# A decode step of grouped-query attention beside a Mish layer: where the mid-run rows of wo are put, and in how many transfers the last eight come

## The chip, the core and the metric

The kernel runs on one core of one Trainium2 chip. The metric is the device time of one execution in microseconds (us); lower is better. A core has TensorE (PE, with its weight loads as PEld), VectorE (DVE), ScalarE (ACT), GpSimd (POOL) and SyncE (SP). SP computes nothing here: it issues almost all of the kernel's DMA transfers, in program order, and waits on semaphores between them. The transfers run on 16 DMA engines that the profile sums up as one row.

## What is computed

One decode step for a batch of 8 with model width 512: layer norm, attention of 32 query heads over 8 cached key and value heads of 8192 positions each, and beside it a dense layer with Mish and a second dense layer. Everything is fp32.

```python
def reference(A_x, A_k_cache, A_v_cache, A_wq, A_wo, B_x, B_w1, B_b1, B_w2):
    xn = _layernorm(A_x, axis=-1)
    # _A_ref: q = xn @ wq, 32 heads of 128; k, v repeated 4 times over the 8 cached heads
    scores = jnp.einsum("bhqd,bhkd->bhqk", q, k) * (Dh ** -0.5)
    o = jnp.einsum("bhqk,bhkd->bhqd", _softmax(scores, axis=-1), v)
    a = o.transpose(0, 2, 1, 3).reshape(B, Sq, Hq * Dh) @ wo
    # _B_ref
    h = jnp.einsum("bsd,df->bsf", xn, w1) + b1
    m = jnp.einsum("bsf,fd->bsd", h * jnp.tanh(softplus(h)), w2)
    return A_x + a + m
```

The caches are the bulk of the data: keys and values are 268 MB each, against 24 MB of weights.

## The kernel before

The work is cut into 32 units (`UNITS`), one for each of 4 pairs of key/value heads (`m`) and each of 8 batch rows (`b`). Unit j loads 8.39 MB of keys and 8.39 MB of values, each as one transfer of 128 partitions by 64 KB (`load_unit`, L136 to L144). Keys have two places in the large tile `kv`, values one (`V_AT`). In step j of the loop (L563 to L604) the PE multiplies the keys of unit j (`scores`), the softmax is made, the PE multiplies the values of unit j-1 (`values`), and then SP is told to load the values of unit j into the place just freed; the keys of unit j+1 are told off in the middle of `scores`. So two to three such transfers are always under way or queued.

The output projection wo is 8.39 MB, 2.1 MB for each pair of heads. It is loaded at the end (L607 to L612) into the place of the last values and keys, as rows of 16 KB in 128 partitions, and used by `outputs`; w2 follows in five pieces (L613 to L619). Of the first pair's wo only three quarters are loaded then (`n = 3 * BW`). The last quarter, 512 KB, comes during the run instead, as 32 rows of 16 KB, into partitions 0 to 11, 32 to 43 and again 0 to 7 of the tile `ws`, which is free once the last part of wq has been used. These rows are the subject:

- `FEW1` (L69) lists eight transfers of three rows, `(p, n, q, at)`: partition, rows, number of the first row, step. With h = 0 or 1 and t = 0 to 3 they are told off two to a step in steps 22 to 25.
- `FEW2` (L70) lists four transfers of two rows, two in step 28 and two in step 29.
- The loop tells them off right behind the step's value load (L591 to L593) by `load_few` (L482 to L488). Row q + 4i goes to partition p + 4i: both sides are walked with a stride of four. A row is four pieces of 4 KB in HBM and one run of 16 KB in its partition.
- `turn_few` (L490) lays the first pair's attention output out in the same order of rows, in unit 9's step. `few(0)` (L508) multiplies the first 44 partitions at the end of step 27 (`EARLY`), before the last eight rows overwrite partitions 0 to 7; `few(1)` multiplies those eight after the loop.

SP's queue is one, so a small transfer stands behind the value load issued just before it and ahead of the next key load.

Of the kernel before, what the change touches and what calls it, by code (L numbers as in the profile page):

```python
# [65 lines left out]

FEW1 = [(32 * h + t, 3, 12 * h + t, 22 + (4 * h + t) // 2) for h in range(2) for t in range(4)]  # L69
FEW2 = [(t, 2, 24 + t, 28 + t // 2) for t in range(4)]  # L70
EARLY = 27


# [4 lines left out]
def kernel(  # L78
# [21 lines left out]
    ws = const.tile([P, CC * BW], F32, name="ws")  # L100
# [381 lines left out]
    def load_few(p, n, q):  # L482

        rows = wo[:4].rearrange("u p f -> (u p f)").rearrange("(u q i f) -> q u i f", u=4, i=4, f=BW)
        nc.sync.dma_start(
            ws[p : p + 4 * n - 3 : 4].rearrange("p (u f) -> p u f", u=4),
            rows[q : q + 4 * n - 3 : 4, :, 3],
        )  # L488

    def turn_few():  # L490
# [72 lines left out]
    for j in range(UNITS):  # L563
# [25 lines left out]
        if j == 0:  # L589
            mish(w1_t, b1_sb, kv[:, W1_AT : W1_AT + 6 * FG])  # L590
        for p, n, q, at in FEW1 + FEW2:  # L591
            if j == at:
                load_few(p, n, q)  # L593
# [14 lines left out]
    for m in range(NP):  # L608
        rows = wo[4 * m : 4 * (m + 1)].rearrange("u p f -> (u p f)")
        rows = rows.rearrange("(p f) -> p f", p=P)  # L610
        n = 3 * BW if m == 0 else 4 * BW
# [4 lines left out]
    for lo, hi in parts:  # L616
        t = kv[:, W2_AT + lo * D : W2_AT + hi * D]
# [64 lines left out]
```

## Time and profile before

| | us |
|---|---|
| median of 3 runs | 1310.62 (1310.28 to 1311.18) |
| profiled execution, its own time | 1310.38 |
| its span, first to last instruction | 1308.6 |
| PE busy | 987.5 |
| DVE busy | 362.0 |
| ACT busy | 39.3 |
| mean rate of the DMA engines | 429 GB/s |

The page gives each engine's busy time, the span in 40 slices, the DMA queues, the chain of work that ended last, and groups of instructions by line. The DMA view of a window counts the packets that start in it: a packet is one contiguous piece on one DMA engine (64 KB for keys and values, 4 KB for the small rows), and the 4-byte packets are the completions that an engine posts when its part of a transfer is done. "Under 512 B" is therefore a count of completions, and "under 8 KB" less "under 2 KB" counts, in the middle of the run, the pieces of the small rows. The share can pass 100% in a short window, since a packet that starts in it is counted whole.

### The profile page before, as it was taken

The numbers are of one execution on the slowest core, as the hardware profiler recorded it, in microseconds if no ns is written. First come the engines' busy times: TensorE is split into PE (matmuls) and PEld (weight loads), VectorE is DVE, ScalarE is ACT, GpSimd is POOL, SyncE is SP. The second block draws the span as 40 slices with busy tenths as digits, with TensorE's granted clock in tenths as the row PEclk, the third lists the DMA queues.
The fourth block names the chain that finished last, engine by engine and source line by source line (L and its number), as shares of the span: only waits on it lengthen the run. The fifth ranks groups of instructions, "written<-read, shape, count | busy, mean of one in ns | idle before, by whom it ended". The sixth has DMA issues, their size and how long they took to land.

```text
span 1308.6 us, 11317 instructions
## 1 busy us (share of the span) xinstructions
PE 987.5 (75%) x5086; PEld 349.0 (27%) x5086; DVE 362.0 (28%) x771; ACT 39.3 (3%) x89; POOL 2.3 (0%) x10
## 2 busy tenths in 40 slices
PE   6967777768878668786878677688796777777677
PEld 4322222223322222232323222232232222222222
DVE  3443022230233332123331232312322330322321
ACT  1000000000000000000000000000000000000000
POOL 0000000000000000000000000000000000000000
PEclk9989888798889899878999888888897898887898
DMA  9999999999999999999999999999999999999997
GB/s 404 441 429 433 433 433 430 431 441 428 435 431 434 433 431 433 431 431 437 425 443 422 443 419 443 429 433 433 426 437 430 438 434 425 441 419 443 423 429 334
DMA packets 11608, 561.80 MB, mean 429 GB/s; under 512 B 1308, under 2 KB 1440, under 8 KB 1960
## 3 DMA queue, kind: packets, MB, share of 16 engines
q1 hardware_dynamic: 11536, 561.06, 99.3%
q8 instruction: 40, 0.66, 0.2%
q14 instruction: 8, 0.07, 0.0%
q10 hardware_dynamic: 24, 0.02, 0.0%
HBM read 561.01 MB, written 0.07 MB: 429 GB/s over the span
## 4 chain that ended last, share of the span: by engine, by line
DMA 79%; PE 20%; issue 0%; SPq 0%; DVE 0%
DMA kv<-in_v 74%; PE o L399 19%; DMA kv<-in_kT 2%; DMA kv<-in_w 2%; DMA kv<-in_wo 2%; PE s L329 1%; PE o L546 0%; SPq L134 0%; DVE os L642 0%
## 5 line engine op out<-in xcount | busy, mean ns | idle before, releaser
L329 PE MATMUL s<-kv,wk 128*64 128x512 f32 x2048 | 502.2, 653 | 180.8 <-DMA kv<-in_kT 180.8
L399 PE MATMUL o<-kv,pt 128*32 128x512 f32 x2048 | 264.5, 675 | 57.4 <-DMA kv<-in_v 57.4
L329 PEld LDWEIGHTS s<-kv,wk 128*64 128x64 f32 x2048 | 164.7, 151 | 495.0 <-issue 413.6
L341 DVE TENSOR_REDUCE nm<-s 128x1 f32<-128x512 f32 x32 | 22.1, 692 | 515.1 <-PE s L329 515.1
L368 PE MATMUL x<-e,perm 128*128 128x512 f32 x256 | 130.1, 655 | 2.0 <-ACT qr L299 2.0
L399 PEld LDWEIGHTS o<-kv,pt 128*32 128x32 f32 x2048 | 69.4, 122 | 226.1 <-issue 175.7
L407 DVE TENSOR_SCALAR os<-o,isel 128x128 f32<-128x128 f32 x32 | 11.2, 351 | 278.2 <-PE o L399 278.2
L379 DVE STREAM_TRANSPOSE tr<-x 128x512 f32<-128x512 f32 x128 | 79.2, 676 | 3.0 <-PE x L368 3.0
L368 PEld LDWEIGHTS x<-e,perm 128*128 128x128 f32 x256 | 50.6, 208 | 74.7 <-issue 72.0
L312 DVE TENSOR_TENSOR wk<-qr,mask 128x512 f32<-128x512 f32 (+1 forms) x66 | 63.5, 1003 | 18.7 <-ACT qr L299 18.7
L360 ACT ACTIVATE e<-s,nmx 128x512 f32<-128x512 f32 x32 | 22.0, 687 | 1119.8 <-DVE nmx L357 1119.8
L388 DVE TENSOR_TENSOR pt<-tr 64x512 f32<-64x512 f32 x64 | 43.9, 686 | 1.6
L384 DVE TENSOR_TENSOR tr<-tr 128x1024 f32<-128x1024 f32 x32 | 39.2, 1226 | 1.1
L409 DVE SCALAR_TENSOR_TENSOR os<-o,isel,os 128x128 f32<-128x128 f32 x96 | 33.7, 351 | 3.4
L342 PE MATMUL m<-ident,nm 128*1 128x128 f32 x32 | 8.6, 270 | 25.3 <-DVE nm L341 25.3
L353 PE MATMUL m<-ident,nx 1*128 1x1 f32 x32 | 7.0, 218 | 24.1 <-DVE nx L349 24.1
L292 PE MATMUL x<-qT,tr 128*128 128x64 f32 x128 | 19.3, 315 | 3.0 <-ACT qr L299 2.7
L292 PEld LDWEIGHTS x<-qT,tr 128*128 128x128 f32 x128 | 18.1, 226 | 6.2 <-ACT qr L299 3.3
L342 PEld LDWEIGHTS m<-ident,nm 128*1 128x1 f32 x32 | 2.5, 79 | 53.5 <-DVE nm L341 53.5
L363 DVE TENSOR_SCALAR lsel<-rsel,l 128x8 f32<-128x8 f32 x32 | 7.4, 231 | 28.8 <-ACT e L360 28.8
L416 PE MATMUL m<-hsel,os 128*128 128x8 f32 x64 | 10.9, 242 | 5.7 <-DVE rt L376 5.7
L416 PEld LDWEIGHTS m<-hsel,os 128*128 128x128 f32 x64 | 10.8, 189 | 15.3 <-issue 8.0
(106 smaller groups left out, 178.8 us busy)
## 6 DMA issues: line engine op xcount, KB each, us to landing
ws<-in_wq SPq DMA_DIRECT2D x4, 2048.0 KB, 22.6
kv<-in_wo SPq DMA_DIRECT2D x3, 2048.0 KB, 24.1
kv<-in_w SPq DMA_DIRECT2D x1, 3584.0 KB, 35.8
kv<-in_wo SPq DMA_DIRECT2D x1, 1536.0 KB
kv<-in_w SPq DMA_DIRECT2D x1, 1280.0 KB
kv<-in_w SPq DMA_DIRECT2D x1, 1024.0 KB
kv<-in_w SPq DMA_DIRECT2D x1, 768.0 KB, 34.9
kv<-in_kT SPq DMA_DIRECT2D x32, 29.4
```

The costliest lines, as they stand in the source:

```text
L292: nc.tensor.matmul(X[:, half, k * 64 : (k + 1) * 64], wide[:, half * 8 + k], qT, start=True, stop=True,)
L312: nc.vector.tensor_mul(w[:, i : i + n, d], q[:, i : i + n, d].to_broadcast([P, n, NH * G, REP]), mask[:, d * NH * G : (d + 1) * NH * G] .r ...
L329: nc.tensor.matmul(S[64 * c : 64 * (c + 1), :], w[:, i].rearrange("p d k h -> p (d k h)"), kk[:, i, c, :], start=(part == 0 and n == 0), s ...
L341: nc.vector.tensor_reduce(nm, S, axis=AX.X, op=ALU.max, negate=True)
L360: nc.scalar.activation(e, S, AF.Exp, bias=nmx, accum_out=l)
L368: nc.tensor.matmul(X[:, g], perm[:, g], e, start=True, stop=True)
L379: nc.vector.transpose(tr.rearrange("p (l t) c -> p t l c", t=TL)[:, tl], X.rearrange("p g (t q l) -> p t l g q", t=TL, q=PP)[:, tl],)
L384: nc.vector.tensor_add(t[:, :, 0], t[:, :, 0], t[:, :, 1])
L388: nc.vector.tensor_add(pt8[half, :, :, d * REP : (d + 1) * REP].rearrange("p c y h -> p y c h"), t[:, 0], t[:, 1],)
L399: nc.tensor.matmul(O[Q * q : Q * (q + 1), :], pt8[:, c, TL * l : TL * (l + 1), :].rearrange("p t h -> p (t h)"), vt[:, 512 * n : 512 * (n ...
L409: nc.vector.scalar_tensor_tensor(os, O[:, DH * i : DH * (i + 1)], isel[:, i : i + 1], os, op0=ALU.mult, op1=ALU.add)
L416: nc.tensor.matmul(M[:, 168 : 168 + H2], os, hsel, start=True, stop=True)
```

## The change

`load_few` walks partitions and rows without a stride: row q + i goes to partition p + i. The lists are rewritten to suit. `FEW1` still has eight transfers of three rows in the same steps, now to three neighbouring partitions. `FEW2` has two transfers of four rows, one in step 28 and one in step 29, each to four neighbouring partitions. Each of the 32 rows goes to the same partition as before, so `turn_few` and `few` stay as they are; which rows share a transfer, and how many transfers there are (ten instead of twelve), is what differs.

```diff
-FEW1 = [(32 * h + t, 3, 12 * h + t, 22 + (4 * h + t) // 2) for h in range(2) for t in range(4)]
-FEW2 = [(t, 2, 24 + t, 28 + t // 2) for t in range(4)]
+FEW1 = [(32 * h + 3 * t, 3, 12 * h + 3 * t, 22 + (4 * h + t) // 2) for h in range(2) for t in range(4)]
+FEW2 = [(4 * t, 4, 24 + 4 * t, 28 + t) for t in range(2)]
...
         rows = wo[:4].rearrange("u p f -> (u p f)").rearrange("(u q i f) -> q u i f", u=4, i=4, f=BW)
         nc.sync.dma_start(
-            ws[p : p + 4 * n - 3 : 4].rearrange("p (u f) -> p u f", u=4),
-            rows[q : q + 4 * n - 3 : 4, :, 3],
+            ws[p : p + n].rearrange("p (u f) -> p u f", u=4), rows[q : q + n, :, 3]
         )
```

## The prediction

> **What bounds the kernel now.** I read the page's DMA rows first, then the chain of waits, then one long window, then the DMA view of short windows around the transfers that change.
>
> ```profile
> span 1308.6 us, 11317 instructions
> ...
> DMA packets 11608, 561.80 MB, mean 429 GB/s; under 512 B 1308, under 2 KB 1440, under 8 KB 1960
> ...
> q1 hardware_dynamic: 11536, 561.06, 99.3%
> ...
> DMA 79%; PE 20%; issue 0%; SPq 0%; DVE 0%
> ```
>
> The chain that ended last is DMA for 79% of the span; the PE pieces in it (20%) are the waits of one value tile for its place. The SP queue's packets fill 99.3% of the time of 16 DMA engines.
>
> ```profile
> core 0: us, PE busy (x) PEld busy (x) DVE busy (x) ACT busy (x) POOL busy (x), PEclk, DMA share, GB/s
> 100.00:1200.00 1100.00, 829.89 (x4176) 289.44 (x4172) 298.55 (x623) 28.80 (x68) 0.00 (x0) 0.88 1.00 433
> ```
>
> Over 1100 us the DMA share is 1.00 at 433 GB/s: none of the 16 engines is ever without work, and one engine moves 433 / 16 = 27.1 GB/s. So the kernel ends when the DMA engine with the most work has done it, and the question is only what the change does to the time that each engine spends.
>
> ```profile
> 917.18 29.90 DMA kv<-in_v
> 947.08 0.04 issue
> 947.12 7.12 PE o L399 x64
> 954.24 0.02 issue
> 954.26 31.52 DMA kv<-in_v
> ```
>
> The chain of waits between 900 and 1000 us shows the cover. A value load of 8.39 MB (128 rows of 64 KB) needs 8.39 / 433 = 19.4 us, but it lands 29.90 us after its issue: some 10.5 us of earlier work stands ahead of it. A late engine therefore always finds its next transfer queued. What it loses is not made good later, and what a leading engine loses costs nothing until it has become the last.
>
> **The transfers that change.** A completion record is 4 bytes, and the page counts 1308 packets under 512 B.
>
> ```profile
> ws<-in_wo SPq DMA_DIRECT2D x8, 48.0 KB
> ws<-in_wo SPq DMA_DIRECT2D x4, 32.0 KB
> ...
> kv<-in_x ACTq DMA_DIRECT2D x1, 16.0 KB
> kv<-in_b ACTq DMA_DIRECT2D x1, 7.0 KB
> ```
>
> 79 transfers of full height on SP's queue (64 of keys and values, 4 of wq, 4 of wo, 1 of w1, 5 of w2, the output) at 16 completions are 1264. x has 8 rows and b1 has 4: 12 more. 1308 - 1264 - 12 = 32 = 8 x 3 + 4 x 2: a small transfer of n rows runs on n engines, one row each. Which engines these are is in no row; I take them to be the same first ones each time, since otherwise no single engine would stand out as it does below.
>
> One row is 16 KB in four pieces of 4 KB, so 16,384 B / 27.1 GB/s = 0.61 us on its engine. Before, engines 0 and 1 take 8 + 4 = 12 such rows each and engine 2 takes 8. After, by counting rows, engines 0 to 2 take 8 + 2 = 10 each, and a fourth engine takes 2.
>
> Now the end. The three lines below are the DMA view's packet counts for 1211 to 1219.7 us, 1219.08 to 1219.66 us and 1304.2 to 1304.8 us.
>
> ```profile
> DMA packets 97, 4.06 MB, mean 467 GB/s; under 512 B 20, under 2 KB 20, under 8 KB 36
> ```
>
> ```profile
> DMA packets 10, 0.41 MB, mean 699 GB/s; under 512 B 1, under 2 KB 1, under 8 KB 4
> ```
>
> ```profile
> DMA packets 7, 0.01 MB, mean 20 GB/s; under 512 B 1, under 2 KB 1, under 8 KB 7
> ```
>
> In the first, all 20 completions of the value load issued at 1189.65 us (16; its row stands below) and of the two small transfers behind it (2 x 2) fall. In the second, the last of the 20 stands alone, with three 4 KB pieces before it: the engine that carries the last small row is the last of all, by about 0.57 us. In the third, again one engine alone still has six 2 KB pieces and a completion of the last weights while the rest are done, again for about 0.57 us (its completion is at the window's end, the others' are before 1304.2). Same lead: **the engine that sets the end is one of the two that carry 12 rows.** What is added to it moves the end one for one; what is taken from it is worth at most 0.57 us.
>
> **The change, part by part.** (1) Two issues fewer on SP.
>
> ```profile
> 1149.15 0.33 SPq L140 DMA_DIRECT2D kv<-in_v  x1
> 1149.53 1.36 SPq L485 DMA_DIRECT2D ws<-in_wo  x2
> 1170.11 0.33 SPq L140 DMA_DIRECT2D kv<-in_kT  x1
> 1189.65 0.33 SPq L140 DMA_DIRECT2D kv<-in_v  x1
> 1190.03 1.33 SPq L485 DMA_DIRECT2D ws<-in_wo  x2
> ```
>
> One issue in place of two saves about 0.7 us of SP at steps 28 and 29, but SP's next instruction of weight, the key load, comes 20 us later and waits for PE: nothing. Were that cover gone, it would be worth 0.7 us each.
>
> (2) When the rows are used.
>
> ```profile
> L511 PE MATMUL h<-ws,oF x32: 587/589/593, 1116.4 to 1289.4; 44*8 44x512 f32 x16, 8*8 8x512 f32 x16
> L485 SPq DMA_DIRECT2D ws<-in_wo x12: 619/706/902, 917.6 to 1190.7; - x12
> ```
>
> ```profile
> DMA packets 64, 1.54 MB, mean 513 GB/s; under 512 B 18, under 2 KB 18, under 8 KB 42
> ```
>
> The last of the first 24 rows move between 1060 and 1063 us (the count above: 42 - 18 = 24 pieces of 4 KB) and are used from 1116.4. The last eight land by 1219.66, and their 16 matmuls of 0.59 us, the last begun at 1289.4, begin near 1280. A delay of some us is covered by 53 and 60 us: nothing. The matmuls read the same partitions as before.
>
> (3) Row counts alone: engines 0 and 1 lose two rows, -1.21 us each, of which the end can feel -0.57.
>
> (4) **Neighbouring partitions.** Before, the rows of one transfer go to partitions t, t+4, t+8; after, to three or four that lie side by side, written by different engines at once. No transfer of this kind of size is in the trace. That several engines are in them at once is seen in 939.9 to 942.4 us, where the first two are moved:
>
> ```profile
> DMA packets 53, 1.15 MB, mean 459 GB/s; under 512 B 13, under 2 KB 13, under 8 KB 37
> ```
>
> 37 - 13 = 24 pieces of 4 KB, 6 rows on three engines in about 2.1 us, where each engine needs 1.21: they overlap, but start up to 0.8 us apart. The lower bound of the price is nothing: rows side by side run as these do. The upper bound is that all rows of a transfer go one after another: 3 x 0.61 for each of FEW1's, so 4 pairs x (6 - 2) x 0.605 = +9.7, and 4 x 0.61 for each of FEW2's two, 4.84 against 2.42 before = +2.4; together +12.1.
>
> The nearest row is x's load, the one in which several engines write side by side (8 rows of 2 KB to partitions 0 to 7). The window 1.69 to 2.7 us holds all its packets:
>
> ```profile
> q1 hardware_dynamic: 14, 0.23, 109.4%
> q10 hardware_dynamic: 15, 0.02, 10.1%
> ```
>
> 10.1% of 16 x 1.01 us is 1.63 us; less 7 completions (under 0.1) that is 0.19 us a row, where 2,048 B / 27.1 is 0.076: 2.6 times. Four writers served in turn at one engine's rate give a mean of (1+2+3+4)/4 = 2.5, eight give 4.5, two 1.5. I take groups of **four partitions that share one path of one engine's rate**. Against it: in the same window the first wq packets, 14 of 16 KB, took 17.7 us, 1.26 each against 0.61, twice as long with no such neighbours, so part of the 2.6 may be the start. It is an estimate from a weak row.
>
> [...]
>
> Worked out: at each of steps 22 to 25 the six rows are partitions 0,1,2 then 3,4,5 (or 6,7,8 then 9,10,11, and the same 32 higher). One group of four gets four rows, 4 x 0.605 = 2.42 us through one path, where each engine now spends 2 x 0.605 = 1.21: +1.21 a step, 4 steps, **+4.8** (taken in full, though the 0.8 us apart may hide a part). At steps 28 and 29 four rows go into one group: 2 x 2.42 = 4.84 against the 4 x 0.605 = 2.42 that engines 0 and 1 spend now, +2.42 if all four arrive together, 2 x 1.82 - 2.42 = +1.2 if three do (the fourth engine's place is not known), -1.21 if none do; with three near each other I take **+1.6**. Sum for the last engine +6.4: 1310.38 (the profiled execution's own time, span 1308.6 and 1.8 around it) + 6.4 = 1316.8. The median of the runs shown, 1310.62, is 0.24 above that execution: **1317.0 us**. Own range 1314.5 to 1318.5.
>
> **Rivals.** *No price for neighbours* (the other side): engines 0 and 1 drop by 1.21, the end by the 0.57 to the next engine: 1310.62 - 0.57 = 1310.05. For it: the pieces now run at full rate with three engines abreast, and the slow first wq packets explain x. Against: x's 2.6.
>
> *A milder path:* if it takes one and a half engines' rate, four rows take 2.42 / 1.5 = 1.61, +0.4 a step, and FEW2 3.23 against 2.42, less what stagger hides: about +1.6 + 0.2, 1312.4. It decides from the moment that two engines abreast already pass 27.1 GB/s.
>
> *A whole transfer on one path:* +12.1, 1322.7. For it nothing but that no row excludes it; x's eight would have shown 4.5.
>
> *The fourth engine becomes the last:* with no price, two new rows (+1.21) on an engine that ends inside the 0.57 us behind the last: up to 1.21 - 0.57 = +0.64, 1311.3. The third line above tells only that the other 15 end before 1304.2; that this one of them is among the latest is possible.
>
> *The change doesn't do what it says:* its words name the last eight rows, but the diff moves all 32 to neighbours; if FEW2's part alone counted, the result would be the -1.21 to +2.42 above.
>
> **How the numbers follow.** Forecast 0.53, no price 0.22, milder 0.13, fourth engine 0.07, whole transfer 0.05. About 0.2% (2.6 us) is what a measurement of this kernel can tell from no change. Slower by more: 0.53 + 0.05 + 0.05 of the milder case = 0.63; within it 0.22 + 0.07 + 0.07 of the milder = 0.36; faster 0.01, since 0.57 us is the most that can be gained. The range 1309.7 to 1318.8 takes in all but the whole-transfer case and a tail of the forecast.
>
> **What would show it.** Right: windows that hold the small transfers (near 940, 980, 1020, 1060 us, then 1178 and 1218) have the same pieces, but over 3 us and more in place of 2.1, with larger shares for fewer bytes; at the end three engines, not one, still run alone, for some 6 us; the mean rate falls to about 427 GB/s; the completions stay 1308 (8 x 3 + 2 x 4 = 32) and L485 has x10. Wrong: pieces still 0.15 us apart on each engine and the end window's lone engine gone, with a time at 1310; then neighbours share nothing. A time above 1319 would mean that they share more than four to a path.

## The result, and the profile after

| | before | changed |
|---|---|---|
| median, 5 runs each (us) | 1310.44 | 1316.07 (1315.65 to 1316.18) |
| span of the profiled execution (us) | 1308.6 | 1314.2 |

The ratio is 1.0042, with a 95% interval from 1.0031 to 1.0053: the change costs 5.6 us. 1317.0 had been forecast, in a range from 1309.7 to 1318.8.

The page of the changed kernel, with the lines that answer to those of before:

```profile
span 1314.2 us, 11315 instructions
...
DMA packets 11608, 561.80 MB, mean 427 GB/s; under 512 B 1308, under 2 KB 1440, under 8 KB 1960
...
q1 hardware_dynamic: 11536, 561.06, 99.2%
...
DMA 78%; PE 21%; issue 0%; SPq 0%; DVE 0%
```

The same 11608 packets and 1308 completions, the same bytes, DMA engines as full as before, but 427 GB/s in place of 429. No waiting time has been added that the page could show as idle; the packets themselves take longer. Where they do is seen in the DMA view of 940.3 to 943.06 us, which holds the first two small transfers:

```profile
DMA packets 52, 1.21 MB, mean 439 GB/s; under 512 B 11, under 2 KB 11, under 8 KB 35
```

35 - 11 = 24 pieces of 4 KB, as in the window shown before, but the last of them begins 2.6 us after the first, where by the same records it was 1.9 before. The packet records of the trace give their durations: the table below has the mean time of one 4 KB piece, the longest, and how many of the 64 KB packets near them took over 2.45 and over 2.9 us (undisturbed they take 2.42). "Near" are those begun from 2.4 us before a step's first piece to 0.1 us after its last began.

```
              first 24 rows    last 8 rows      64 KB packets near them
              mean   longest   mean   longest   all   over 2.45   over 2.9   (pieces in ns, packets in us)
before        161    172       162    172       159     0          0
changed       231    509       198    501       213   103          7
```

Pieces that took 161 ns take up to 509, about three times as long, and around them half of the big packets are late too, most of them by about 0.1 us (the median of the late ones is 2.53). The last stretch of the run, from 1304.70 us to the last completion of the weights, by the view of windows (busy time by engine, then clock, DMA share and rate):

```profile
core 0: us, PE busy (x) PEld busy (x) DVE busy (x) ACT busy (x) POOL busy (x), PEclk, DMA share, GB/s
1304.70:1310.38 5.68, 3.54 (x88) 1.90 (x88) 0.00 (x0) 0.58 (x1) 0.00 (x0) 1.00 0.19 77
```

A share of 0.19 of 16 engines is 3.0 engines in the mean, but not three all the time. The DMA view of 1307.66 to 1310.38 us, and then of 1309.72 to 1310.38 us:

```profile
q1 hardware_dynamic: 47, 0.12, 11.1%
```

```profile
q1 hardware_dynamic: 9, 0.02, 6.4%
```

6.4% of 16 is one engine, and 11.1% is 1.8: two, and then the one. By the packet records nine are still at work at 1305.0 us and three from 1305.7 us on. Before, one engine was alone for the last 0.57 us; now at most three are at work for the last 4.7 us, at most two for the last 2.7 us and one for the last 0.66 us. And the issues of the small transfers:

```profile
L485 SPq DMA_DIRECT2D ws<-in_wo x10: 246/298/338, 917.7 to 1194.8; - x10
```

Ten instead of twelve, as listed, and each one shorter (298 ns in place of 706), which SP, waiting for other things, makes nothing of.

### The profile page after: what moved, and what is told of

It reads as the page before. It is cut to its first block, busy times and chain, and to the rows that moved or that the text cites. A ratio compares the mean times of both kernels' runs of the same rounds, so it can differ in the third digit from the quotient of the medians.

```text
span 1314.2 us, 11315 instructions
## 1 busy us (share of the span) xinstructions
PE 1000.5 (76%) x5086; PEld 350.3 (27%) x5086; DVE 362.0 (28%) x771; ACT 39.3 (3%) x89; POOL 2.3 (0%) x10
## 2 busy tenths in 40 slices
DMA packets 11608, 561.80 MB, mean 427 GB/s; under 512 B 1308, under 2 KB 1440, under 8 KB 1960
## 3 DMA queue, kind: packets, MB, share of 16 engines
q1 hardware_dynamic: 11536, 561.06, 99.2%
## 4 chain that ended last, share of the span: by engine, by line
DMA 78%; PE 21%; issue 0%; SPq 0%; DVE 0%
DMA kv<-in_v 73%; PE o L399 20%; DMA kv<-in_kT 2%; DMA kv<-in_w 2%; DMA kv<-in_wo 2%; PE s L329 1%; PE o L545 0%; SPq L134 0%; DVE os L641 0%
## 5 line engine op out<-in xcount | busy, mean ns | idle before, releaser
L329 PE MATMUL s<-kv,wk 128*64 128x512 f32 x2048 | 508.1, 659 | 178.0 <-DMA kv<-in_kT 170.6
L399 PE MATMUL o<-kv,pt 128*32 128x512 f32 x2048 | 273.4, 694 | 52.0 <-DMA kv<-in_v 52.0
```

What stands on the lines that cost most here:

```text
L329: nc.tensor.matmul(S[64 * c : 64 * (c + 1), :], w[:, i].rearrange("p d k h -> p (d k h)"), kk[:, i, c, :], start=(part == 0 and n == 0), s ...
L399: nc.tensor.matmul(O[Q * q : Q * (q + 1), :], pt8[:, c, TL * l : TL * (l + 1), :].rearrange("p t h -> p (t h)"), vt[:, 512 * n : 512 * (n ...
```

## The experiments

Ten kernels ran, in three groups, each with its own runs of the kernel before beside it (medians 1310.41, 1310.39 and 1310.49 us). `load_few` was given two strides, `ps` for partitions and `qs` for rows in HBM, so that the two sides could be changed apart; where a row comes to another partition, the lists in `turn_few` and `few` were changed to suit. The copies that this adds cost nothing that shows: four of the kernels that have them stay at the time of before (1309.93 to 1310.38 us).

```diff
-    def load_few(p, n, q):
+    def load_few(p, n, q, ps, qs):
...
+            ws[p : p + ps * (n - 1) + 1 : ps].rearrange("p (u f) -> p u f", u=4),
+            rows[q : q + qs * (n - 1) + 1 : qs, :, 3],
```

**Which of the two lists costs?** The first 24 rows changed alone:

```diff
+FEW1 = [(32 * h + 3 * t, 3, 12 * h + 3 * t, 22 + (4 * h + t) // 2, 1, 1) for h in range(2) for t in range(4)]
+FEW2 = [(t, 2, 24 + t, 28 + t // 2, 4, 4) for t in range(4)]
```

> Only the first 24 rows go to neighbouring partitions (three rows each, as in the changed kernel); the last eight stay as before. Theory 'neighbouring partitions share one path': most of the +5.6 us of the change, +4 to +5 over before, pieces of 4 KB at 0.3 to 0.5 us near 940, 981, 1022 and 1062 us and at 0.16 us near 1178 and 1218. Rival 'the last eight rows in two transfers cost it': within 1 us of before.

Measured: 1314.88 us, +4.5, ratio 1.0034 (1.0022 to 1.0047). The pieces of the first 24 rows take 237 ns in the mean, those of the last eight 167. Then the last eight alone:

```diff
+FEW1 = [(32 * h + t, 3, 12 * h + t, 22 + (4 * h + t) // 2, 4, 4) for h in range(2) for t in range(4)]
+FEW2 = [(4 * t, 4, 24 + 4 * t, 28 + t, 1, 1) for t in range(2)]
```

> Only the last eight rows go by two transfers of four neighbouring partitions; the first 24 stay as before. Theory 'neighbouring partitions share one path': between -0.6 (the engines do not meet) and +1.6 us over before. Rival 'the last eight rows in two transfers cost it': +4 us or more.

Measured: 1312.53 us, +2.1, ratio 1.0016 (1.0008 to 1.0025): more than the upper end expected, and far below the rival. The pieces of these eight rows take 299 ns in the mean and up to 625. So most of the cost lies in the new places of the first 24 rows, which still come in eight transfers of three, and less in the last eight, whose transfers become fewer.

**HBM or SBUF?** Each side was put next to each other alone, with the number of transfers and the rows of every engine as before.

```diff
+FEW1 = [(32 * h + t, 3, 12 * h + 3 * t, 22 + (4 * h + t) // 2, 4, 1) for h in range(2) for t in range(4)]
+FEW2 = [(t, 2, 24 + 2 * t, 28 + t // 2, 4, 1) for t in range(4)]
```

> The rows of a transfer lie side by side in HBM (16 KB apart in place of 64 KB), but go to partitions four apart as before. Theory 'neighbouring partitions share one path': within 0.5 us of before, all pieces at 0.16 us. Rival 'rows that lie side by side in HBM are read one after another': +4 us or more, with long pieces.

Measured: 1310.38 us, ratio 0.9999 (0.9990 to 1.0008), the pieces at 161 and 162 ns in the mean, no 64 KB packet near them over 2.45 us.

```diff
+FEW1 = [(32 * h + 3 * t, 3, 12 * h + t, 22 + (4 * h + t) // 2, 1, 4) for h in range(2) for t in range(4)]
+FEW2 = [(2 * t, 2, 24 + t, 28 + t // 2, 1, 4) for t in range(4)]
```

> The rows of a transfer lie 64 KB apart in HBM as before, but go to neighbouring partitions, three (first 24 rows) or two (last eight) at a time, with the row counts of each transfer as before. Theory 'neighbouring partitions share one path': +4 to +6 us, pieces at 0.3 to 0.5 us. Rival 'rows that lie side by side in HBM are read one after another': within 0.5 us of before.

Measured: 1317.19 us, +6.8, ratio 1.0052 (1.0039 to 1.0065), pieces at 241 and 242 ns. The cost is wholly on the SBUF side. It is above the upper end expected (+6), and above the changed kernel's, whose busiest engines take ten rows and not twelve; that this is the whole reason was not tried.

**Neighbours, or other partitions?** All rows stay four apart, with the transfers and row counts of before, but 12 partitions higher (12 to 23, 44 to 55, then 12 to 19):

```diff
+FEW1 = [(32 * h + 12 + t, 3, 12 * h + t, 22 + (4 * h + t) // 2, 4, 4) for h in range(2) for t in range(4)]
+FEW2 = [(12 + t, 2, 24 + t, 28 + t // 2, 4, 4) for t in range(4)]
```

> [...] Theory 'only small rows side by side get in each other's way': within 0.5 us of before, pieces at 0.16 us. [...]

Measured: 1317.53 to 1322.21 us in five runs, median 1321.93, +11.5; the ratio, 1.0079 (1.0066 to 1.0091), is that of the means (1320.83 here). The profile is of the fastest of the five, +7.1; why they differ by 4.7 us was not tried. No two rows of a transfer are neighbours, and it is the slowest of all; the theory that only small rows side by side disturb each other falls. Two lines of the view of windows, 936 to 946 us, first of before, then of this kernel:

```profile
936.00:946.00 10.00, 8.46 (x40) 2.83 (x36) 1.32 (x5) 0.00 (x0) 0.00 (x0) 1.00 0.96 416
```

```profile
936.00:946.00 10.00, 8.06 (x38) 2.69 (x34) 1.47 (x6) 0.12 (x1) 0.00 (x0) 1.00 0.98 370
```

The engines are as busy (0.96 and 0.98), and move 370 GB/s in place of 416. The packet records show how: the first pieces of a step take 160 to 200 ns, the later ones settle near 325, half the rate. Of the 149 big packets near the small rows, 124 are over 2.45 us and 92 over 2.9, where none of the 159 of before is over 2.45: the big loads lose as well. Half the rate is what one path shared by two would give. That the other one on it is the stream of 64 KB packets is an estimate from these numbers: which engine writes which partitions is in no record.

**How far does a path reach?** The last eight rows in four transfers of two, with the second row 32 partitions from the first in place of four:

```diff
+FEW2 = [(t, 2, 24 + t, 28 + t // 2, 32, 4) for t in range(4)]
```

> The first 24 rows as before; the last eight in four transfers of two as before, but the two rows of a transfer are 32 partitions apart (t and 32 + t) in place of four. Theory 'the path is that of four consecutive partitions': within 0.5 us of before. [...]

Measured: 1312.62 us, +2.2, ratio 1.0017 (1.0008 to 1.0026). The pieces of these rows go from 162 to 207 ns in the mean, again first 160 and then some 310. It is not the place by itself: partitions 32 to 35 take rows of the first 24 in this same kernel, as the first rows of their transfers, at 161 ns. What differs is the engine that writes there.

The records show whom it meets. A packet begins 3 or 4 ns before the one ahead of it on its engine ends, so the packets of one engine can be linked. In step 28 one engine writes its two small rows, 160 ns a piece, and goes on with a 64 KB packet that begins at 1178.716 us and takes 3.56 us. The other engine's long pieces, from 1178.910 to 1180.417 us, all fall into that packet. Step 29 shows the same, with 3.63 us. So the second engine's small rows, 32 partitions up, and the first one's big packet are slow at the same time, where my theory of four consecutive partitions had expected no change. The records name no partition: whether p and p + 32 are on one path, or on two that the same engine fills, was not shown.

**Eight rows in one transfer**, four apart and then side by side:

```diff
+FEW2 = [(0, 8, 24, 28, 4, 1)]
```

> The first 24 rows as before; the last eight in one transfer of eight rows four partitions apart (0, 4, ... 28), one row for each of eight engines. Theory 'each engine has a path of its own there': no long pieces, the last engine loses three rows (12 to 9) but the next one ends 0.57 us behind it, so -0.3 to -0.6 us against before. Rival 'more engines in one small transfer cost more': +1 us or more.

Measured: 1310.30 us, ratio 0.9999 (0.9990 to 1.0008). No long piece (160 ns in the mean, 167 at most), but 0.1 us of gain where 0.3 to 0.6 had been expected. The DMA view of this kernel for 1180.45 to 1180.69 us:

```profile
DMA packets 4, 0.14 MB, mean 563 GB/s; under 512 B 1, under 2 KB 1, under 8 KB 2
```

The last completion of step 28's loads is again that of a small row, with the row's last 4 KB piece before it. Linked as above, the packets ahead of it have no other small row in them: one of the eight engines was among the latest without any, and the one that it now gets makes it the last.

```diff
+FEW2 = [(0, 8, 24, 28, 1, 1)]
```

> As the spread transfer of eight rows, but to eight neighbouring partitions (0 to 7); row counts of every engine and the transfer's size are the same, only the spacing differs. Theory 'four consecutive partitions share one path': two groups of four, each row 2.4 us in place of 0.6, +1 to +2.5 us over the spread one. Rival 'all rows of a transfer share one path': eight rows at 4.8 us, +4 us or more. Rival 'spacing does not matter at eight rows': equal to the spread one.

Measured: 1311.53 us, ratio 1.0008 (0.9999 to 1.0016), 1.2 us above the spread transfer. Pieces at 215 ns in the mean and up to 545. It is the low end of what was expected, and excludes one path for a whole transfer; the interval against before just touches 1.

**Is it the two transfers of four rows?** The change's own split of the last eight, with the same rows for every engine, but four partitions apart:

```diff
+FEW2 = [(t, 4, 24 + 4 * t, 28 + t, 4, 1) for t in range(2)]
```

> The last eight rows in two transfers of four, as the change has them, with the same rows for each engine (10, 10, 10, 2), but to partitions four apart (0, 4, 8, 12 and 1, 5, 9, 13); the first 24 as before. Theory 'only the place in SBUF costs': -0.6 to +0.2 us against before, no long pieces, some 2 us below the run with neighbouring partitions. Rival 'two transfers of four rows cost more by themselves': +1.5 us or more.

Measured: 1310.02 us against 1310.49 beside it, ratio 0.9996 (0.9988 to 1.0005), pieces at 160 ns. Its rows fall in the same steps as those of the run with the last eight alone as neighbours, which stands at +2.1. The DMA share and rate of 1174 to 1188 us are where the difference shows, first this run, then that run with neighbours:

```profile
1174.00:1188.00 14.00, 11.87 (x74) 3.32 (x74) 1.71 (x7) 0.78 (x2) 0.00 (x0) 0.88 0.94 407
```

```profile
1174.00:1188.00 14.00, 10.27 (x62) 2.92 (x62) 1.71 (x7) 0.78 (x2) 0.00 (x0) 0.88 0.98 389
```

407 GB/s at a share of 0.94 is 433 for engines that are always busy, as over the long window of before; 389 at 0.98 is 397. Two transfers in place of four cost nothing; the place does.

**The 0.57 us at the end.** Rows shared out 11, 11 and 10 over three engines, four partitions apart:

```diff
+FEW2 = [(0, 3, 24, 28, 4, 1), (1, 3, 27, 28, 4, 1), (2, 2, 30, 29, 4, 1)]
```

> The first 24 rows as before; the last eight in transfers of three, three and two rows, four partitions apart, so that three engines take 11, 11 and 10 rows in place of 12, 12 and 8. Theory 'the end is set by an engine with 12 rows, 0.57 us ahead of the next': -0.3 to -0.6 us against before, no long pieces. Rival 'another engine ends with it anyway': within 0.2 us of before.

Measured: 1309.93 us against 1310.49, ratio 0.9996 (0.9987 to 1.0005). The medians differ by 0.56 us, as worked out, but the interval has 1 in it: it may be the fastest of all these kernels, and by this measurement it is not told apart from before.

## Why the prediction was right

*The bound.* DMA engines that are hardly ever idle (99.3% before, 99.2% after), and an end that the engine with most work sets: borne out. With the same bytes and the same number of packets the time grew, and it grew on few engines: the forecast had three of them alone at the end for some 6 us, and three, then two, then one are at work for the last 4.7 us. The small pieces of a step were to take 3 us and more in place of 2.1; in steps 22 to 25 they took 2.7, 3.0, 3.3 and 3.6 us. That the three engines at the end are the ones with ten rows is not seen in its records.

*Row counts.* The prediction took the small rows to be always on the same first engines. Linked as above, the records bear this out in three kernels: 12, 12 and 8 rows on three engines before, 11, 11 and 10 in the run of that name, and 10, 10, 10 and 2 in the run four apart, with no small row on any other engine. In the others some links are open, since two engines can end a packet within 1 ns of each other. Gains at the end limited to 0.57 us: the two kernels that take rows from the busiest engines and keep them four partitions apart came out 0.56 and 0.47 us lower, in line but within noise. The eight-row transfer gained next to nothing, since it gave a row to an engine that was already late; that is the prediction's "fourth engine" rival in another place. For the change's own fourth engine it did not come true: 10, 10, 10 and 2 rows four apart are not slower.

*The two terms.* The sum of +6.4 came out as +5.6. The first 24 rows were put at +4.8 and measured +4.5 alone. The last eight were put at +1.6 and measured +2.1 alone, within the stated ends of -1.2 and +2.4. Together they are 6.6, 1 us more than the change costs: in the changed kernel the last eight rows' pieces take 198 ns, against 299 when only they are neighbours. The records show why that may be: in step 28 the four engines begin their rows at 1179.5, 1181.2, 1181.9 and 1184.5 us, spread by what the earlier rows cost them, where alone they all begin within about 1 us. That this spread explains the whole difference of 1 us was not tried.

*The reason for the price.* Here the step was only half right, and that the sum came near is partly luck. "Groups of four partitions that share one path of one engine's rate" has about the right rate: 12 partitions higher the pieces settle near 325 ns in place of 161. But small rows do not only slow each other. By the step as it was written, the run 12 partitions higher would have cost nothing, since no two engines write small rows into one group of four there; it cost the most, and 92 of the 149 big packets near its rows took over 2.9 us. So rows four apart do not run freely because they are not neighbours. In the run 32 apart, too, no two engines write small rows into one group of four in steps 28 and 29, and one engine's pieces of some 310 ns lie in another's 64 KB packet of 3.56 us, in place of 2.42. The reading that fits both runs is that a row is slow where it meets another engine's big packets. It is an estimate from them: no record names an engine or a partition, and whose big packets go to which partitions was not shown. Of rows four apart that begin at partitions 0 to 3 and 32 to 35, the runs show only that their pieces stay near 161 ns.

The durations of the pieces can be set beside the extra time (mean of one 4 KB piece in ns; a dash: no figure):

```
kernel                       first 24 rows   last 8 rows   us over before
11/11/10                           -              -            -0.6
four apart                         -             160           -0.5
spread8                            -             160           -0.1
HBM side by side                  161            162            0.0
eight side by side                 -             215           +1.1
last 8 as neighbours               -             299           +2.1
32 apart                           -             207           +2.2
first 24 as neighbours            237            167           +4.5
changed                           231            198           +5.6
SBUF side by side                 241            242           +6.8
12 partitions higher           160 to 200, then near 325       +7.1 to +11.8
```

Of the kernels with a mean, those with none above 162 ns are at the time of before, and those with longer pieces above it (the eight side by side only just). The durations do not give the price: eight rows at 299 ns cost +2.1 us, and eight at 207 ns +2.2.

*The rivals.* "No price for neighbours" falls with the two runs that change one side each. "A milder path" falls with the pieces that settle at half rate, some 325 ns in place of 161. "A whole transfer on one path" falls with the eight rows side by side. What the x load was taken to show, four writers in turn, agrees with the longest piece where four rows are neighbours (625 ns, 3.9 times 161), but it stays the weak row that it was called.

## What to carry to other kernels

Where DMA engines are full (99.3% here), a small transfer is not free by its bytes: with the same transfers of the same 512 KB, the place alone made it 1310.39 us or up to 1322.21. The rows 12 partitions higher ran at half the rate (near 325 ns a piece in place of 161), and the big loads were held up as well (92 of 149 packets near them over 2.9 us). Try more than one place: here rows four apart that begin at partitions 0 to 3 and 32 to 35 cost nothing, the same 12 partitions higher the most. And look at the duration of single packets, since the busy share hardly tells (0.96 before, 0.98 in the slowest kernel, 936 to 946 us). When one edit moves two groups of rows, change each alone: here the group that kept its number of transfers cost twice as much as the one that did not.

## What was not expected

The harm does not stay with the engines that meet. When only the last eight rows are neighbours, 41 of the 146 big packets near them take over 2.45 us, 23 of them over 2.9; at 1221.2 us sixteen late packets are under way at once, as many as there are engines, though four engines write the rows; with HBM alone side by side there are none in 152. The runs show late packets, not what makes them late.

The issue of a transfer to neighbouring partitions is shorter whatever the HBM side does: 276 ns in the median with rows 64 KB apart in HBM, 298 in the changed kernel, against 706 and 707 four partitions apart. Here nothing waits for it.
